# Issuing the loads of all later batches from GpSimd instead of SyncE, and reordering the first batch's hand-over

## The chip, the cores and the metric

The kernel runs on one core of one Trainium2 chip. The metric is device time in microseconds (us) of one execution. Three runs of the kernel before gave 276.81, 277.83 and 279.06 us; the median, 277.83 us, is the time before.

The engines are named as in the profile: PE is TensorE's matrix multiplier and PEld its weight load, DVE is VectorE, ACT is ScalarE, POOL is GpSimd, SP is SyncE. A "q" behind a name (SPq, POOLq) is the engine's instruction queue, from which it also issues transfers. Transfers that SP issues run in the hardware queue q1, transfers that POOL issues in the software queue q0; both share the same 16 DMA engines.

## What is computed

A linear attention with cosine weights, and then a mixer that mixes over positions and over channels. There are 8 batches of 8 heads, 576 positions and 64 elements per head.

```python
def phi(x, c, s):                       # c, s: cos and sin of pi/2 * position / 576
    r = np.maximum(x, 0.0)
    return np.concatenate([r * c, r * s], axis=-1)
q_p, k_p = phi(q, cos_w, sin_w), phi(k, cos_w, sin_w)
kv  = einsum('bhsf,bhsd->bhfd', k_p, v)
num = einsum('bhsf,bhfd->bhsd', q_p, kv)
den = einsum('bhsf,bhf->bhs', q_p, k_p.sum(axis=2)) + 1e-06
x = (num / den)                         # heads side by side: (8, 576, 512)
h = relu(x^T @ w_tok1) @ w_tok2         # over positions, 256 wide
u = x + h^T
out = u + relu(u @ w_ch1) @ w_ch2       # over channels, 1536 wide
```

All inputs and the output are float32; the kernel multiplies in bfloat16.

## The kernel before

**Tiles.** The 576 positions of a batch are four chunks of 128 (0 to 3) and a tail of 64, called chunk R (4). Two batches share the 128 partitions of a tail tile, so the tail's features, u and channel part are computed for both batches of a pair at once, with the odd one. The chunks of a batch are worked in the order 0, 1, 2, R, 3 (`ORDER`).

**Two halves of the work.** `Front` holds what a batch needs up to u: features of k and q (`feature`, line 264, on DVE), values cast to bfloat16 (`values`, lines 275 and 277), the products kv (`kv`, line 321), the turned query features (`q_trans` with PE for the first two batches, `q_trans_dma`, line 353, a transposing transfer from SP, for the others), the numerators (`num`, line 362), the token mixer (`tok1`, line 385, and `tok2`, line 409), and the turning of u (`u_trans_dma`, line 438, and `tail_trans_dma`, line 443, transfers from SP). `Channel` holds the channel mixer: 12 steps of `c_main` (line 531) with `c_tail` (line 551) in odd batches, and then the steps of `o_step` (line 564), two of the 12 blocks of `w_ch2` at a time.

**Order of the work.** The order is written by hand: every engine takes its instructions in program order, and waits only for data and for buffers that are still in use. While `Channel(b)` runs through its steps, the pieces of `Front(b + 1)` are put between them: `pieces` makes a list of (step, piece). Step C + i is the i-th of the 12 `c_main` steps, O + i the i-th `o_step` behind them. For a batch from the third on, chunks' query features and their transposes stand at steps C + 1 to C + 5, the numerators at C + 8 to O + 3, then the mixer and the transposes of u. The first batch is worked alone (`first_front`), and the second batch's pieces, which use PE transposes, stand between the channel steps of the first (`first` in `pieces`, lines 468 to 481). There the last piece list holds the query transposes of chunks 2, R, 3 with three of the first batch's `tok2` between them, the casts of v (two on POOL, two on ACT, one on DVE) and kv.

**Loads.** A main load of k, v or q of a batch is 1,024 KB (`load_main`, line 86), a load of a tail 128 KB (`load_tail`, line 92). Main tiles have two buffers (`io`, `bufs=2`), so batch b + 2 goes where batch b was. `load_batch` issues them on SP: those of batch 1 at the start, the first of them behind the second of the `w_ch1` loads (an added dependency, `after`); k and v of batch 2 at step 12 of the first channel behind the second `w_ch2` load, and q of it 16 steps later; in steady state v and q of batch b + 2 at step 5 of channel b, and k of batch b + 3 at step 24 (step 30 for b = 0). As SP takes its instructions in order, they go out only when the transposes and stores that stand ahead of them in the program have gone out. An even batch brings the tails of its pair with it. The weights `w_ch1` and `w_ch2` are loaded from POOL, which casts them on the way (lines 188 and 194); `w_ch2` waits for q of batch 1. The stores are issued by SP (lines 571 and 575).

Of the kernel before, what the change touches and what calls it, by code (L numbers as in the profile page):

```python
# [16 lines left out]
def kernel(  # L17
# [15 lines left out]
    nc = tc.nc  # L33

    B, H, S, D = q.shape
# [4 lines left out]
    P = 128  # L40
    R = S // P
# [5 lines left out]
    NCH = D_ch // P  # L47
# [9 lines left out]
    def half(g):  # L57
        return slice(g * ST, (g + 1) * ST)
# [19 lines left out]
    def after(later, earlier):  # L78
        tc.add_manual_dep(later.ins, earlier.ins.name,
                          mybir.DependencyInfo(mybir.DependencyClass.Sync,  # L80
                                               mybir.DependencyReason.DATA),
                          reason="order of the first loads")


    def load_main(dst, src, b, lo=0, hi=H, eng=nc.sync):
        return eng.dma_start(
            out=dst[:, lo:hi, 0:R * D].rearrange("p h (r d) -> p h r d", r=R),
            in_=src[b, lo:hi, 0:SM, :].rearrange("h (p r) d -> p h r d", r=R))


    def load_tail(dst, src, b):
        return nc.sync.dma_start(out=dst[half(b % 2)],
                                 in_=src[b, :, SM:S, :].rearrange("h s d -> s h d"))

    def tiles():
        return tuple(io.tile([P, H, R * D], F32, name=n) for n in ("qt", "vt", "kt"))

    def tail_tiles():
        return tuple(io.tile([P, H, D], F32, name=n) for n in ("qtt", "vtt", "ktt"))
# [4 lines left out]
    load_main(qt0, q, 0, 0, HH)  # L104
    load_main(qt0, q, 0, HH, H, nc.scalar)
    load_tail(qtt0, q, 0)
    load_main(kt0, k, 0, 0, HH)
    k_done = load_main(kt0, k, 0, HH, H)
    load_tail(ktt0, k, 0)
    load_main(vt0, v, 0, 0, HH)  # L110
    load_tail(vtt0, v, 0)
    load_main(vt0, v, 0, HH, H)

# [11 lines left out]
    w_ch2 = const.tile([P, NCH, Dm], BF16, name="w_ch2")  # L125
# [59 lines left out]
    w_ch1_done = []  # L185
    for c2 in range(2):
        for ki in range(0, NCC, 2):
            w_ch1_done.append(nc.gpsimd.dma_start(
                out=w_ch1[:, ki:ki + 2, c2 * C2:(c2 + 1) * C2],
                in_=moe_w_ch1[ki * P:(ki + 2) * P, c2 * C2:(c2 + 1) * C2]  # L190
                .rearrange("(n c) d -> c n d", c=P)))
    after(w_ch1_done[0], k_done)
    def load_w_ch2(behind):
        done = [nc.gpsimd.dma_start(
            out=w_ch2[:, ki:ki + 4, :],
            in_=moe_w_ch2[ki * P:(ki + 4) * P, :].rearrange("(n t) d -> t n d", t=P))
            for ki in range(0, NCH, 4)]
        after(done[0], behind)
        return done

# [14 lines left out]
    class Front:  # L217
# [243 lines left out]
        def pieces(self, b, before):  # L461


            first, odd = b == 1, b % 2 == 1
            V, KV, N = self.values, self.kv, self.num
            KS, QS, QT, T = self.k_side, self.q_side, self.q_trans, self.tok2
            C, O = 0, NCH
            if first:

                last = NCH - 1  # L470
                plan = [(4, KS, 0), (5, KS, 1, True), (6, KS, 2, True), (6, KS, 3, True), (7, KS, R),
                        (8, QS, 0), (9, QS, 1), (9, QT, 0), (10, QS, 2), (10, QT, 1)]
                plan += [(last, *what) for what in (
                    (QS, 3, True), (QT, 2, (0, H), nc.vector), (before.tok2, 2, None, False),
                    (QS, R, True), (QT, 3), (before.tok2, 3, None, False),
                    (QT, R, (0, H), nc.vector), (before.tok2, R, None, False))]
                plan += [(last, V, ci, eng) for ci, eng in enumerate(
                    (nc.gpsimd, nc.gpsimd, nc.scalar, nc.scalar, nc.vector))]
                plan += [(last, KV, ci) for ci in range(NSC)]
                plan.append((last, self.kv_out))  # L480
                plan += [(5, before.tok2, 0, ps_at, False), (7, before.tok2, 1, ps_at, False)]
            else:
                plan = [(C + at, V, ci, nc.scalar) for ci, at in enumerate((-1, -1, 0, 1, 2))]
                plan += [(C + at, KS, ci) for ci, at in enumerate((0, 0, 1, 2, 2))
                         if ci < R or not odd]
                for ci, at in zip(ORDER, (1, 2, 3, 4, 5)):
                    if ci < R or not odd:
                        plan += [(C + at, QS, ci), (C + at, self.q_trans_dma, ci)]

                plan += [(C + at, KV, ci) for ci, at in  # L490
                         enumerate((2, 3, 4, 5, 6) if odd else (2, 3, 4, 6, 7))]
                plan.append((C + (6 if odd else 7), self.kv_out))
            if first:
                at, mix, t = (O + 1, O + 3, O + 5, O + 7, O + 9), O + 10, O + 14
            elif odd:
                at, mix, t = (C + 8, C + 9, C + 11, O + 1, O + 3), O + 4, O + 8
            else:
                at, mix, t = (C + 9, C + 10, C + 11, O + 1, O + 3), O + 4, O + 8
            plan += [(i, N, ci) for i, ci in zip(at, ORDER)]
            plan += [(mix, self.mix_head, 0), (mix + 1, self.mix_head, 1),  # L500
                     (mix + 2, self.mix_tail)]

            plan += [(t + at, T, ci) for ci, at in enumerate((0, 1, 2, 3, 3) if not first else
                                                             (0, 0, 1, 2, 2))]
            plan += [(t + 3 - first, self.u_trans_dma, 3, R)]
            plan.append((t + 2 - first, self.u_trans_dma, 0, 3))
            if odd:
                plan.append((t + 3 - first, self.tail_trans_dma))
            slots = {}
            for slot, what, *args in sorted(plan, key=lambda p: p[0]):  # L510
                slots.setdefault(slot, []).append((what, args))
            return slots
# [183 lines left out]
                c.c_block(mi, kb)  # L696
        return c

    def load_batch(b, which="kvq", behind=None):
        if b not in io_tiles:  # L700
            io_tiles[b] = tiles()
        if b // 2 not in io_tails:
            io_tails[b // 2] = tail_tiles()
        qt, vt, kt = io_tiles[b]
        qtt, vtt, ktt = io_tails[b // 2]
        done = []
        for n in which:
            dst, tail_dst, src = {"k": (kt, ktt, k), "v": (vt, vtt, v), "q": (qt, qtt, q)}[n]
            done.append(load_main(dst, src, b))
            if behind is not None and len(done) == 1:  # L710
                after(done[0], behind)
            if b % 2 == 0:
                load_tail(tail_dst, src, b)
            if b % 2 == 0 or b == 1:
                load_tail(tail_dst, src, b | 1)
        return done


    results = [dict() for _ in range(B)]
    done = load_batch(1, "kqv", behind=w_ch1_done[1])  # L720
    w_ch2_done = load_w_ch2(done[1])
    tails = {0: tail0}
    f = Front(0, results[0], tail0)
    c = first_front(f)
    for b in range(B):
        slots = {}
        if b + 1 < B:
            if (b + 1) // 2 not in tails:
                tails[(b + 1) // 2] = Tail((b + 1) // 2)
            slots = Front(b + 1, results[b + 1], tails[(b + 1) // 2]).pieces(b + 1, f)  # L730
        if b > 0:
            c = Channel(b, results[b], tails[b // 2])
        for what, args in slots.pop(-1, ()):
            what(*args)
        for i, step in enumerate(c.steps(AHEAD if b == 0 else 0)):
            step()
            for what, args in slots.pop(i, ()):
                what(*args)


            if b == 0 and i == NCH:
                load_batch(2, "kv", behind=w_ch2_done[1])
            if b == 0 and i == NCH + 16:
                load_batch(2, "q")
            if 0 < b < B - 2 and i == NSC:
                load_batch(b + 2, "vq")
            if b < B - 3 and i == NCH + (18 if b == 0 else 12):
                load_batch(b + 3, "k")
        assert not slots
# [32 lines left out]
```

## Time and profile before

| what | value |
|---|---|
| runs (median; lowest, highest) | 277.83 us; 276.81, 279.06 |
| profiled execution | 275.45 us, of which the span of the profile is 273.6 |
| granted clock of PE | 1.0 of full speed, in all 40 slices |
| PE busy | 261.6 us, 96% of the span, 2050 matmuls |
| DVE, ACT, POOL busy | 164.7, 129.8, 11.2 us |
| DMA queue q1 (from SP) | 49.62 MB, 65.4% of 16 engines' span |
| DMA queue q0 (from POOL) | 3.21 MB, 7.1% |

PE's busy time is a poor gauge here: the rows give a 128x512 matmul about 379 ns, but back to back they start every 216 ns. What PE loses shows as distance between starts beyond that. The stages of the span are: the first batch's front to about 26 us, the first channel with the second batch's pieces to about 60 us, and from there one channel in each 27 to 34 us, the last of which ends at 270 us and is followed by the last stores.

### The profile page before, as it was taken

What the parts mean: (1) busy time and instruction counts of PE and PEld (TensorE: products, weight loads), DVE (VectorE), ACT (ScalarE), POOL (GpSimd) and SP (SyncE); (2) the same over time, 40 slices, a digit from 0 to 9 for tenths busy, and PEclk for the clock granted to TensorE, in tenths of its full rate; (3) what the DMA queues carried; (4) which work ended last, traced back from release to release, by engine and by line L of the source; (5) the groups of instructions that cost most, each with busy time, mean ns of one, the idle gap of its engine ahead of it and who ended that gap; (6) DMA issues with size and microseconds to landing.
All of it is one profiled execution on the core that took longest, in us unless ns stands there. A gap on an engine that the chain in (4) does not pass through costs nothing.

```text
span 273.6 us, 5130 instructions
## 1 busy us (share of the span) xinstructions
PE 261.6 (96%) x2050; PEld 138.7 (51%) x2050; DVE 164.7 (60%) x375; ACT 129.8 (47%) x229; POOL 11.2 (4%) x24
## 2 busy tenths in 40 slices
PE   7989987999899999999999999999999999999994
PEld 2665354446554454445654455446644455435543
DVE  6973775774876396659566487659466577720022
ACT  4955982067525184156626183347606372426500
POOL 6400230000000000000000000000000000000000
PEclk9999999999999999999999999999999999999999
DMA  7999999738995897968993969669994361180032
GB/s 222 344 266 283 317 179 283 245 88 264 284 253 185 247 221 191 323 140 233 208 311 79 270 193 259 220 151 237 211 304 119 115 117 38 42 210 0 2 98 94
DMA packets 91816, 53.68 MB, mean 196 GB/s; under 512 B 59409, under 2 KB 86929, under 8 KB 91793
## 3 DMA queue, kind: packets, MB, share of 16 engines
q1 hardware_dynamic: 88432, 49.62, 65.4%
q0 software_dynamic: 2832, 3.21, 7.1%
q10 hardware_dynamic: 528, 0.52, 0.6%
q8 instruction: 16, 0.26, 0.4%
q14 instruction: 8, 0.06, 0.1%
HBM read 35.85 MB, written 9.44 MB: 166 GB/s over the span
## 4 chain that ended last, share of the span: by engine, by line
PE 80%; DMA 7%; DVE 7%; ACT 2%; issue 1%; SPq 0%; DVEq 0%
PE o_ps L564 31%; PE c_ps L531 23%; PE b_ps L385 6%; PE u_ps L409 5%; PE num_ps L362 4%; PE ct_ps L551 4%; DMA qpT<-qp 4%; PE kv_ps L321 3%; DVE qp L264 2%; DMA uT<-u_bf 2%; DMA qt<-in_q_dram 2%; DVE kp L264 2%; PE idle_ps L205 1%; PE c_ps L541 1%; DVE u_sb L412 1%
## 5 line engine op out<-in xcount | busy, mean ns | idle before, releaser
L564 PE MATMUL o_ps<-w_ch,h1T 128*128 128x512 bf16 (+1 forms) x396 | 94.8, 372 | 0.0
L531 PE MATMUL c_ps<-uT,w_ch 128*128 128x512 bf16 (+2 forms) x384 | 91.6, 372 | 1.0 <-DMA uT<-u_bf 1.0
L535 ACT ACTIVATE h1T<-c_ps 128x512 bf16<-128x512 f32 x93 | 55.4, 598 | 57.1 <-PE c_ps L531 56.9
L564 PEld LDWEIGHTS <-h1T 128*128 128x128 bf16 x396 | 37.0, 97 | 38.8
L531 PEld LDWEIGHTS <-w_ch 128*128 128x128 bf16 x384 | 33.3, 97 | 31.2 <-DMA uT<-u_bf 2.0
L569 DVE TENSOR_TENSOR o_sb<-o_ps,u_sb 128x512 f32<-128x512 f32 (+1 forms) x33 | 22.2, 673 | 32.7 <-PE o_ps L564 32.7
L412 DVE TENSOR_TENSOR u_sb<-u_ps,x_sb 128x512 f32<-128x512 f32 x32 | 22.0, 689 | 7.3 <-PE u_ps L409 6.8
L416 ACT CAST u_bf<-u_sb 128x512 bf16<-128x512 f32 x28 | 17.3, 618 | 17.8 <-DVE u_sb L412 16.1
L390 ACT ACTIVATE B<-b_ps 128x512 bf16<-128x512 f32 x8 | 4.8, 597 | 39.5 <-PE b_ps L385 39.5
L409 PE MATMUL u_ps<-B,w_tok 128*128 128x512 bf16 x80 | 22.5, 379 | 0.0
L372 DVE TENSOR_TENSOR x_sb<-num_ps,den 128x512 bf16<-128x512 f32 x28 | 19.4, 691 | 1.0
L551 PEld LDWEIGHTS <-w_ch 128*128 128x128 bf16 x192 | 14.0, 98 | 9.2
L264 DVE TENSOR_SCALAR qp<-qt,cos_t 128x512 bf16<-128x512 f32 (+1 forms) x35 | 15.9, 453 | 4.6 <-DMA qt<-in_q_dram 4.6
L385 PE MATMUL b_ps<-x_sb,w_tok 128*128 128x512 bf16 x64 | 17.9, 379 | 0.0
L264 DVE TENSOR_SCALAR kp<-kt,cos_t 128x512 bf16<-128x512 f32 x32 | 15.2, 480 | 3.9 <-DMA kt<-in_k_dram 3.9
L551 PE MATMUL ct_ps<-uT_tail,w_ch 128*128 128x128 bf16 x192 | 17.2, 219 | 0.0
L275 ACT CAST v_aug<-vt 128x512 bf16<-128x512 f32 (+1 forms) x30 | 16.7, 586 | 0.1
L264 DVE TENSOR_SCALAR qp<-qt,sin_t 128x512 bf16<-128x512 f32 (+1 forms) x34 | 15.7, 460 | 0.0
L362 PEld LDWEIGHTS <-qpT 128*128 128x128 bf16 x256 | 11.5, 98 | 7.1 <-DMA qpT<-qp 1.5
L362 PE MATMUL num_ps<-kv_sb,qpT 128*128 128x65 bf16 x256 | 13.1, 193 | 1.7 <-DMA qpT<-qp 0.7
L569 DVE TENSOR_TENSOR o_sb<-o_ps,u_tail 128x512 f32<-128x512 f32 x4 | 2.8, 692 | 20.0 <-PE o_ps L564 20.0
L321 PE MATMUL kv_ps<-v_aug,kp 128*128 128x65 bf16 x256 | 12.5, 193 | 2.2 <-ACT v_aug L275 1.7
(96 smaller groups left out, 220.9 us busy)
## 6 DMA issues: line engine op xcount, KB each, us to landing
out_dram<-o_sb SPq DMA_DIRECT2D x31, 256.0 KB, 2.9
kt<-in_k_dram SPq DMA_DIRECT2D x7, 1024.0 KB, 6.9
qt<-in_q_dram SPq DMA_DIRECT2D x7, 1024.0 KB, 8.6
vt<-in_v_dram SPq DMA_DIRECT2D x7, 1024.0 KB, 6.5
w_ch<-in_moe_w_ch_dram POOLq DMA_DIRECT2D x4, 384.0 KB, 10.4
w_ch<-in_moe_w_ch_dram POOLq DMA_DIRECT2D x3, 512.0 KB, 8.3
out_dram<-o_sb SPq DMA_DIRECT2D x10, 128.0 KB, 2.3
qtt<-in_q_dram SPq DMA_DIRECT2D x8, 128.0 KB, 5.9
```

Of the source, the lines that this page charges most:

```text
L264: nc.vector.tensor_scalar(o_ap, i_ap, scalar1=w, scalar2=0.0, op0=ALU.mult, op1=ALU.max)
L321: nc.tensor.matmul(self.kv_ps[g][:, j * DP:j * DP + D1], self.k_of(ci)[:, g * HH + j, :, :] .rearrange("p a b -> p (a b)"), self.va[:, ci, ...
L362: nc.tensor.matmul(num_ps[:, g, j * DP:j * DP + D1], self.qT_of(ci, h), self.kv_sb[g][:, j, 0:D1], start=True, stop=True)
L372: nc.vector.tensor_mul(self.x_of(ci)[rows].rearrange("p (g j d) -> p g j d", g=2, j=HH), nv[:, :, :, 0:D], den.to_broadcast([rows.stop - r ...
L385: nc.tensor.matmul(self.b1_ps[mi], w, self.x_of(ci), start=(ci == ORDER[0]), stop=(ci == ORDER[-1]))
L409: nc.tensor.matmul(u_ps, w_tok2[:, ki, ci * P:(ci + 1) * P], self.B1[:, ki, :], start=(ki == 0), stop=(ki == NT - 1))
L412: nc.vector.tensor_add(u, u_ps[rows], self.x_of(ci)[rows])
L531: nc.tensor.matmul(c_ps[:, lo:hi], w_ch1[:, ki, mi * P:(mi + 1) * P], uT[:, lo // P:hi // P, ki, :], start=(ki == 0), stop=(ki == NCC - 1))
L535: nc.scalar.activation(self.h1T[:, mi, :], c_ps, AF.Relu)
L551: nc.tensor.matmul(self.ct_ps[:, mi % R, :], w_ch1[:, ki, mi * P:(mi + 1) * P], self.tail.uT[:, ki, :], start=(mi % R == 0 and ki == 0), s ...
L564: nc.tensor.matmul(o_ps, h, w_ch2[:, ki, cols], start=ki == 0, stop=ki == NCH - 1)
L569: nc.vector.tensor_add(o_sb, o_ps, u)
```

## The change

- `load_batch` issues every load of batches 1 to 7, tails too, on POOL's queue. SP keeps the loads of batch 0, two weight loads, all transposes and all stores.
- The three added dependencies of these loads go: k of batch 1 behind the second `w_ch1` load, `w_ch2` behind q of batch 1, and k of batch 2 behind the second `w_ch2` load. On POOL's queue they follow each other in program order. The dependency of the first `w_ch1` load on k of batch 0 stays.
- q of batch 2 is issued with k and v of it, 16 steps earlier in the program.
- For the second batch, the query transposes of chunks 0 and 1 move from steps 9 and 10 behind step 11, so that all stand behind the first batch's `tok2` of chunks 2 and 3; the first batch's `tok2` of its tail moves behind kv; four chunks of v are cast on POOL (two before), none on ACT; chunk 1's and 3's transposes are copied out on DVE.
- For batches 3, 5 and 7 (counted from 0), the numerators of chunks 2, R and 3, the mixer and u's transposes stand one step earlier.

```diff
-    def load_tail(dst, src, b):
-        return nc.sync.dma_start(out=dst[half(b % 2)],
+    def load_tail(dst, src, b, eng=nc.sync):
+        return eng.dma_start(out=dst[half(b % 2)],
...
-    def load_w_ch2(behind):
...
-        after(done[0], behind)
+    def load_w_ch2():
...
                 plan = [(4, KS, 0), (5, KS, 1, True), (6, KS, 2, True), (6, KS, 3, True), (7, KS, R),
-                        (8, QS, 0), (9, QS, 1), (9, QT, 0), (10, QS, 2), (10, QT, 1)]
+                        (8, QS, 0), (9, QS, 1), (10, QS, 2), (10, QS, 3, True)]
                 plan += [(last, *what) for what in (
-                    (QS, 3, True), (QT, 2, (0, H), nc.vector), (before.tok2, 2, None, False),
-                    (QS, R, True), (QT, 3), (before.tok2, 3, None, False),
-                    (QT, R, (0, H), nc.vector), (before.tok2, R, None, False))]
-                plan += [(last, V, ci, eng) for ci, eng in enumerate(
-                    (nc.gpsimd, nc.gpsimd, nc.scalar, nc.scalar, nc.vector))]
+                    (QS, R, True), (before.tok2, 2, None, False), (before.tok2, 3, None, False),
+                    (QT, 0), (QT, 1, (0, H), nc.vector), (QT, 2), (QT, 3, (0, H), nc.vector),
+                    (V, R, nc.vector), (QT, R, (0, H), nc.vector))]
+                plan += [(last, V, ci, nc.gpsimd) for ci in range(R)]
                 plan += [(last, KV, ci) for ci in range(NSC)]
-                plan.append((last, self.kv_out))
+                plan += [(last, self.kv_out), (last, before.tok2, R, None, False)]
...
             elif odd:
-                at, mix, t = (C + 8, C + 9, C + 11, O + 1, O + 3), O + 4, O + 8
+                at, mix, t = (C + 8, C + 9, C + 10, C + 11, O + 2), O + 3, O + 7
...
-            done.append(load_main(dst, src, b))
-            if behind is not None and len(done) == 1:
-                after(done[0], behind)
+            load_main(dst, src, b, eng=nc.gpsimd)
             if b % 2 == 0:
-                load_tail(tail_dst, src, b)
+                load_tail(tail_dst, src, b, nc.gpsimd)
             if b % 2 == 0 or b == 1:
-                load_tail(tail_dst, src, b | 1)
+                load_tail(tail_dst, src, b | 1, nc.gpsimd)
...
-    done = load_batch(1, "kqv", behind=w_ch1_done[1])
-    w_ch2_done = load_w_ch2(done[1])
+    load_batch(1, "kqv")
+    load_w_ch2()
...
             if b == 0 and i == NCH:
-                load_batch(2, "kv", behind=w_ch2_done[1])
-            if b == 0 and i == NCH + 16:
-                load_batch(2, "q")
+                load_batch(2, "kvq")
```

More of the change, by code (lines that the diff above doesn't have):

```diff
@@ L192 @@
     after(w_ch1_done[0], k_done)
-    def load_w_ch2(behind):
[L194 to L197, printed above, removed]
-        after(done[0], behind)
-        return done
+    def load_w_ch2():
+        for ki in range(0, NCH, 4):
+            nc.gpsimd.dma_start(
+                out=w_ch2[:, ki:ki + 4, :],
+                in_=moe_w_ch2[ki * P:(ki + 4) * P, :].rearrange("(n t) d -> t n d", t=P))
     def busy(dst, times):
@@ L697, in first_front, with load_batch @@
         return c
-    def load_batch(b, which="kvq", behind=None):
+    def load_batch(b, which="kvq"):
         if b not in io_tiles:
@@ L705, in load_batch @@
         qtt, vtt, ktt = io_tails[b // 2]
-        done = []
         for n in which:
             dst, tail_dst, src = {"k": (kt, ktt, k), "v": (vt, vtt, v), "q": (qt, qtt, q)}[n]
-            done.append(load_main(dst, src, b))
-            if behind is not None and len(done) == 1:
-                after(done[0], behind)
+            load_main(dst, src, b, eng=nc.gpsimd)
             if b % 2 == 0:
-                load_tail(tail_dst, src, b)
+                load_tail(tail_dst, src, b, nc.gpsimd)
             if b % 2 == 0 or b == 1:
-                load_tail(tail_dst, src, b | 1)
-        return done
+                load_tail(tail_dst, src, b | 1, nc.gpsimd)
     results = [dict() for _ in range(B)]
-    done = load_batch(1, "kqv", behind=w_ch1_done[1])
-    w_ch2_done = load_w_ch2(done[1])
+    load_batch(1, "kqv")
+    load_w_ch2()
     tails = {0: tail0}
```

## The prediction

> **What bounds the kernel now.** I read the stretches by stage first, to see where PE is short of work, then PE's waits, then the chain of work, and last the transfers of single windows. PE's clock is 1.0 throughout, so it plays no part.
>
> ```profile
> 28.00:49.00 21.00, 17.89 (x172) 10.03 (x171) 15.22 (x35) 13.46 (x22) 3.88 (x5) 1.00 1.11 263
> 49.00:77.00 28.00, 26.44 (x229) 14.92 (x228) 19.02 (x42) 14.31 (x26) 0.00 (x0) 1.00 0.79 214
> 77.00:238.00 161.00, 160.87 (x1181) 82.60 (x1178) 105.94 (x237) 73.83 (x131) 0.00 (x0) 1.00 0.73 196
> ```
>
> The columns are the stretch, its length, and PE's busy time first. From 77 to 238 us PE lacks 0.13 us. There the kernel is bound by PE's own work, and better transfers can win almost nothing. What can be won lies in 28 to 77 us (3.1 + 1.6 us idle). The waits and the chain name the causes:
>
> ```profile
> PE kv_ps L321 <- ACT v_aug L275: 1.7, 1, 1.7
> PE qT_ps L343 <- DVE qp L264: 1.3, 2, 0.7
> PE c_ps L531 <- DMA uT<-u_bf: 1.0, 2, 0.6
> PE num_ps L362 <- DMA qpT<-qp: 0.7, 1, 0.7
> ```
> ```profile
> 42.38 1.05 ACT v_aug L275 x2
> 57.21 3.30 DMA uT<-u_bf
> 68.25 5.41 DMA qpT<-qp
> 100.74 4.42 DMA qpT<-qp
> ```
>
> The reader sees one stall on ACT's casts of v, some on query features, and transposes that the chain holds as late. A transpose lands a median 3.0 us after its issue; the one of 68.25 took 5.41, behind k of batch 3 in q1 (issued at 64.05, landed at 71.57).
>
> **Time base.** The profiled execution took 275.45 us (span 273.6 and 1.85 around it), 2.38 below the median of 277.83. Differences are worked out on its trace and added to the median.
>
> **What the change saves.** (1) In the second batch's pieces PE's starts show 0.84 (34.44 us), 0.82 (38.76), 1.82 (42.95) and 0.28 us (43.47) of waiting: 3.8. With the transposes after `tok2` and the casts on POOL these go, but five PE transposes now follow each other through two PSUM buffers, each copied out in 1.0 us (ACT) or 0.69 (DVE): about 0.85 + 0.7 + 0.7 us of new waiting. Saved: 1.5. POOL's four casts take 4 x 0.72 = 2.9 us from v's landing (35.98), so to 38.9, before kv at about 40.8; this hides them by 1.9 us. (2) Batch 2's q lands at 67.28 because it is issued at 61.30; loaded early it removes 0.55 us (69.03) and 0.91 (73.70): 1.45. (3) u of the last batch a step earlier takes about 0.45 of the 0.78 us at 243.8. Sum: 3.4 us. SP loses 42 load issues of 0.4 to 3.6 us; PE is not waiting for them beyond (2).
>
> **What it adds: issue on POOL.** 21 tails at about 0.65 us and 21 main loads at about 1 us (estimates from POOL's own rows: 0.60 us for a load of 64 packets, 0.80 for 256, 0.83 for 512): some 35 us, on an engine with 11.2 us of work. Only the casts of v stand behind loads there, behind `w_ch2`. If POOL can't write the 6,000 packets of batch 1 and `w_ch2` ahead, the casts start only when the third `w_ch2` load is let in, up to 3 us after they are wanted; the trace shows no more than the 1,024 of `w_ch1` written ahead. The bounds are 0 and 3 us. I take 0, since PE has 1.9 us in hand there and what is ahead drains at the same time as v, and keep 3 for the range.
>
> **What it adds: loads that run ahead.** SP's order held the loads back: v and q of batch 5 went out at 134.71, behind the transposes of 126.71 to 133.40. POOL has nothing ahead of them but a free buffer. In channel b the buffers of batch b + 1 come free when its features are made: in channel 2, k at 99.67 and q at 102.04, v before. So k, v, q of batch b + 3, 3 MB (3.75 with tails), start in q0 at 101 us, just when batch b + 1's transposes of 98.95, 100.74, 102.1 and 103.4 are in q1. Before they met only an earlier load; now all but the first share the engines with 9 to 11 us of loads. This occurs in channels 1 to 4; channels 5 and 6 load nothing.
>
> How the two queues share: here both had long rows of packets, and transposes alone:
>
> ```profile
> q0 software_dynamic: 167, 0.26, 62.2%
> q1 hardware_dynamic: 172, 0.38, 47.9%
> ```
> ```profile
> GB/s 272 127 18 94 0 0 0 0 0 0 214 152 246 269 257 255 164 44 18 18 18 9 0 0 0 3 9 6 12 9 9 9 12 9 20 260 284 287 295 281
> q1 hardware_dynamic: 1199, 0.30, 92.5%
> q8 instruction: 1, 0.02, 2.4%
> ```
>
> The first fence is 14.75 to 17 us: 167 packets against 172, one for one whatever their size. The second is 101 to 104.5 us: one 16 KB packet of another queue (1.4 us on one engine) takes the whole transpose stream from 270 GB/s to about 10. [...]
>
> A transpose is 1,024 rows of 256 B, 64 on each engine at 18 ns: 1.15 us. A 1 KB load packet takes 46 ns. One for one, a transpose takes 64 x 64 ns = 4.1 us; unslowed 1.15. I take 3 rows per 2 load packets, 3.1 us: near the one-for-one row, the only one with two full queues, but less, as q0's packets first moved 1.4 to 4.2 us after issue and leave gaps. Channel 2, with transposes wanted by the numerators at 103.8, 104.9, 106.0 and 108.3 (the last two a step earlier than the 107.19 and 109.40 seen): the first lands unslowed at 101.8, the others at 105.45, 108.55, 111.65, so PE waits 0.55 + 2.0 + 0.8 = 3.35 us (each wait moves what follows). Channel 4 the same. Channels 1 and 3 have slack, since their numerators come later and tails' packets take only 18 ns: 1.55 each, all at chunk 3. Sum 9.8. Before that, batches 2 and 3 now queue behind `w_ch2` to about 64 us (6.75 MB at 330 GB/s from 44), so u's first transpose at 57 us, 96 rows, takes 4.7 us instead of 1.7: 2.9 more at the 0.6 us wait of 60.55. Total added 12.7; net 12.7 - 3.4 = +9.3: 287.1.
>
> [...]
>
> **The rivals.** A, the other side: transposes travel in long turns. If 16 rows (288 ns) go between 4 load packets (184 ns), a transpose takes 4 x 472 ns = 1.9 us; channel 2 waits 0.15, u 1.1, and the savings stand: -3.4 + 1.4 = -2.0, 275.8; with no slowing at all 274.4. It decides from 2.2 us per transpose downwards. For it: 256 B packets of q1 went several to one of q0 around 9 us; against it: the one-for-one window. B: strictly one for one: waits of 5.5, 5.5, 3.9, 3.9 and 4.4: +23.2 - 3.4 = 297.6. C: POOL's writing of packets blocks DVE's features. Seen: of nine around POOL's 2.48 us at 32.6, two took 0.6 instead of 0.48 us. That is 0.25 us; at a whole issue (0.8 us) for each of six features it is 4.8, less 1.65 us of slack, in 4 channels: +12.6 - 3.4 = 287. [...] D: late casts, A with 3 us more: 278.
>
> **How the numbers follow.** Forecast (transposes slowed, 279 to 296) 0.54; A 0.25; B and beyond 0.10; C 0.05; D 0.06. The time is the forecast's, 287.1; its own range 279 to 296. A range that leaves 2 in 10 out takes in A's near end and stops at B: 274.5 to 297.6. A difference under 1% can't be told from none (275.05 to 280.61). Faster: most of A, 0.20. Same: the rest of A, D, the forecast's low end, 0.18. Slower 0.62.
>
> **What would show it.** Right: transposes of channels 1 to 4 landing 4 to 9 us after issue, waits of numerators on them, loads of batch b + 3 in the first third of channel b, none of this in channels 5 and 6. PE's wait on ACT's v gone. Wrong: transposes at 3 us beside full q0 (A); loads that start only late in a channel, for POOL waits I overlooked; features at 1 us (C).

## The result and the profile after

The kernel after takes 326.17 us (median of its three fast runs, 324.71 to 327.41; 329.18 over all six, of which three, at 330.94 to 333.95, fell into a slower state that runs of any kernel can fall into) against 277.61 us before (6 runs, 275.97 to 279.06). The ratio is 1.175, 95% interval 1.167 to 1.183. The forecast was 287.1 us and its range ended at 297.6, so the sign was right and the size was not. The profiled execution took 326.17 us, of which the span is 324.0.

Here are the stretches by stage of the kernel after, the last one longer because the kernel is. Columns as before: stretch, length, busy time of PE, PEld, DVE, ACT and POOL, then PE's clock, the DMA share and GB/s.

```profile
28.00:49.00 21.00, 19.35 (x187) 11.14 (x185) 17.74 (x38) 11.92 (x19) 11.15 (x15) 1.00 1.10 289
49.00:77.00 28.00, 19.28 (x124) 10.04 (x122) 15.16 (x33) 9.29 (x17) 9.98 (x10) 0.82 1.06 290
77.00:290.00 213.00, 181.81 (x1272) 91.38 (x1271) 109.66 (x245) 79.80 (x143) 20.10 (x18) 0.91 0.57 136
```

The first stretch gained: PE is busy for 19.35 us of it where it was 17.89. The second lost 7.2 us of PE's work, and from 77 us on PE is idle for 31 us where it lacked 0.13. There is also something new in the clock's column: 0.82 and 0.91 where the kernel before shows 1.00. PE's waits, and POOL's longest one (who waited for what: total us, times, longest):

```profile
PE num_ps L360 <- DMA qpT<-qp: 20.0, 5, 6.8
PE num_ps L360 <- DMA qpT_tail<-qp_tail: 11.1, 2, 6.8
PE c_ps L528 <- DMA uT<-u_bf: 8.7, 1, 8.7
PE qT_ps L341 <- ACT qpT L345: 1.1, 1, 1.1
```
```profile
POOL kt L86 <- DVE kp L262: 117.9, 4, 38.0
```

PE's wait on ACT's casts of v is gone, and in its place are 1.1 us on a copy out of PSUM, where this kernel's matmuls write. All other new waits above 0.5 us are for transposes. POOL's longest waits, 117.9 us in all, are for a free buffer, as foreseen; its others are 6 us or less. The chain of waits (start, length, what) holds the same transposes, now 11 to 21 us long where those shown of before took 3.3 to 5.4:

```profile
76.76 13.67 DMA qpT_tail<-qp_tail
...
117.07 11.43 DMA qpT<-qp
...
158.21 20.84 DMA qpT<-qp
...
206.01 14.16 DMA qpT<-qp
```

The transfers of 122 to 129 us, in the second half of the second of these, by queue (packets, MB, share of 16 engines' time):

```profile
q0 software_dynamic: 620, 2.40, 93.2%
q1 hardware_dynamic: 625, 0.15, 10.6%
```

The reader sees three things. The queues share one packet for one, 620 to 625 (some 30 of each are of 4 B). A packet of q0 is 2.40 MB / 620 = 3.9 KB, and takes 0.932 x 16 x 7 us / 620 = 168 ns; a row of q1 takes 19 ns. And 625 rows in 7 us make 7 x 1024 / 625 = 11.5 us for one transpose. The packet records give most of q0's packets 4,096 B and 164 ns, and 64 x (18 + 164) ns is 11.6 us. The forecast had 3.1.

Between PE's matmul starts I count 41.6 us of waiting on transposes: 8.9 us for u (ended 67.5), 4.8 in channel 1 (84.9 and 90.5), 7.25 in channel 2 (120.5 and 128.55), 14.0 in channel 3 (170.1 and 179.1), 6.65 in channel 4 (214.7 and 220.2), and none in channels 5 and 6. Behind the six waits of 4.5 us and more, 128x512 matmuls start every 427 ns instead of 216 (behind the first, 128x384 ones every 320 instead of 163), for 1.3 to 5.1 us each; this loses another 11.0 us in these large matmuls, 12.7 with the small ones. The page's clock row shows the same dips:

```profile
PEclk9999999859959998799985599959999999999999
```

### The profile page after: what moved, and what is told of

The parts are those of the page before. It is cut to its first block, busy times and chain, and to the rows that moved or that the text cites. A ratio compares the mean times of both kernels' runs of the same rounds, so it can differ in the third digit from the quotient of the medians.

```text
span 324.0 us, 5146 instructions
## 1 busy us (share of the span) xinstructions
PE 276.5 (85%) x2050; PEld 143.9 (44%) x2050; DVE 166.0 (51%) x376; ACT 127.6 (39%) x226; POOL 58.3 (18%) x68
## 4 chain that ended last, share of the span: by engine, by line
PE 72%; DMA 19%; SPq 3%; DVE 3%; ACT 1%; issue 1%; POOL 0%; POOLq 0%
PE o_ps L561 29%; PE c_ps L528 19%; DMA qpT<-qp 14%; PE b_ps L383 6%; PE u_ps L407 5%; DMA qpT_tail<-qp_tail 4%; PE idle_ps L203 3%; SPq L351 3%; PE num_ps L360 3%; PE kv_ps L319 2%; PE ct_ps L548 2%; PE qT_ps L341 1%; DVE kp L262 1%; PE c_ps L538 1%; DVE qp L262 1%
## 5 line engine op out<-in xcount | busy, mean ns | idle before, releaser
L528 PE MATMUL c_ps<-uT,w_ch 128*128 128x512 bf16 (+2 forms) x384 | 95.7, 385 | 8.7 <-DMA uT<-u_bf 8.7
L561 PE MATMUL o_ps<-w_ch,h1T 128*128 128x512 bf16 (+1 forms) x396 | 99.8, 388 | 0.0
L561 PEld LDWEIGHTS <-h1T 128*128 128x128 bf16 x396 | 38.6, 101 | 42.6 <-issue 5.0
L528 PEld LDWEIGHTS <-w_ch 128*128 128x128 bf16 x384 | 34.5, 101 | 40.3 <-DMA uT<-u_bf 9.2
L86 POOL DMA_DIRECT2D kt<-in_k_dram x7 | 15.7, 2245 | 118.2 <-DVE kp L262 117.9
L360 PE MATMUL num_ps<-kv_sb,qpT 128*128 128x65 bf16 x256 | 13.9, 200 | 21.0 <-DMA qpT<-qp 20.0
L368 DVE TENSOR_SCALAR den<-num_ps 128x8 f32<-128x8 f32 (+1 forms) x35 | 5.8, 166 | 50.5 <-PE num_ps L360 50.4
L360 PEld LDWEIGHTS <-qpT 128*128 128x128 bf16 x256 | 11.9, 102 | 28.3 <-DMA qpT<-qp 23.1
L383 PE MATMUL b_ps<-x_sb,w_tok 128*128 128x512 bf16 x64 | 19.9, 415 | 0.0
L548 PEld LDWEIGHTS <-w_ch 128*128 128x128 bf16 x192 | 14.0, 98 | 9.2
L262 DVE TENSOR_SCALAR qp<-qt,cos_t 128x512 bf16<-128x512 f32 (+1 forms) x35 | 16.2, 462 | 0.6 <-DMA qt<-in_q_dram 0.6
L273 ACT CAST v_aug<-vt 128x512 bf16<-128x512 f32 (+1 forms) x28 | 15.7, 589 | 0.1
```

What stands on the lines that cost most here:

```text
L262: nc.vector.tensor_scalar(o_ap, i_ap, scalar1=w, scalar2=0.0, op0=ALU.mult, op1=ALU.max)
L360: nc.tensor.matmul(num_ps[:, g, j * DP:j * DP + D1], self.qT_of(ci, h), self.kv_sb[g][:, j, 0:D1], start=True, stop=True)
L383: nc.tensor.matmul(self.b1_ps[mi], w, self.x_of(ci), start=(ci == ORDER[0]), stop=(ci == ORDER[-1]))
L528: nc.tensor.matmul(c_ps[:, lo:hi], w_ch1[:, ki, mi * P:(mi + 1) * P], uT[:, lo // P:hi // P, ki, :], start=(ki == 0), stop=(ki == NCC - 1))
L548: nc.tensor.matmul(self.ct_ps[:, mi % R, :], w_ch1[:, ki, mi * P:(mi + 1) * P], self.tail.uT[:, ki, :], start=(mi % R == 0 and ki == 0), s ...
L561: nc.tensor.matmul(o_ps, h, w_ch2[:, ki, cols], start=ki == 0, stop=ki == NCH - 1)
```

## The experiments

My theory after the result (T): GpSimd's loads of batch b + 3 run beside the transposes of batch b + 1, q0's packets are 4 KB, the queues take turns packet by packet, and so a transpose takes some 11 us; the long waits then halve PE's clock. Rivals: the new order of the work is the cause (O); GpSimd's own work or queue is, by something other than its packet size (G).

**Keep the change, take the collision away.** The first load of each group from batch 3 on waits for the last transpose issued ahead of it. Nothing else changes.

```diff
+    turned = []
...
+            turned.append(nc.sync.dma_start_transpose(...))
...
-            load_main(dst, src, b, eng=nc.gpsimd)
+            done = load_main(dst, src, b, eng=nc.gpsimd)
+            if at == 0 and turned:
+                after(done, turned[-1])
```

> The changed kernel, with all loads from batch 3 on still issued by GpSimd, but the first of each group held until the last transpose issued ahead of it has landed. Theory T (turns): two queues take turns packet by packet on each DMA engine, and a packet of GpSimd's loads is 4,096 B (164 ns) against a transpose's row of 256 B (18 ns), so a transpose beside loads lands 10 us late; without the overlap transposes land about 3 us after issue, the waits of 41.6 us and the half clock of 11 us behind them go, and the time is 273 to 277 us. [...]

Measured: 274.09 us (272.12 to 274.82); ratio to before 0.988, interval 0.985 to 0.992. PE's waits on transposes in it, its last long stretch, and POOL's longest wait:

```profile
PE num_ps L362 <- DMA qpT<-qp: 0.8, 2, 0.4
PE c_ps L530 <- DMA uT<-u_bf: 0.7, 1, 0.7
```
```profile
77.00:238.00 161.00, 160.16 (x1163) 81.96 (x1162) 106.08 (x233) 74.34 (x132) 19.68 (x25) 1.00 0.76 195
```
```profile
POOL vt L86 <- DMA qpT<-qp: 41.2, 3, 15.2
```

POOL now waits for transposes, where nothing depends on it, and PE does not. The whole loss is gone, half clock included. The two profiled executions differ by 326.17 - 274.02 = 52.15 us; the waits (41.6 less the 1.5 left here) and the half clock (11.0) explain 51.1 of them, or 52.8 with the small matmuls at half clock. It also shows what the rest of the change is worth: 277.15 - 274.09 = 3.06 us.

**The new order alone.** The loads stay on SP as before; only the order of the second batch's pieces and the earlier step for odd batches are taken over.

```diff
-                        (8, QS, 0), (9, QS, 1), (9, QT, 0), (10, QS, 2), (10, QT, 1)]
+                        (8, QS, 0), (9, QS, 1), (10, QS, 2), (10, QS, 3, True)]
...
-                at, mix, t = (C + 8, C + 9, C + 11, O + 1, O + 3), O + 4, O + 8
+                at, mix, t = (C + 8, C + 9, C + 10, C + 11, O + 2), O + 3, O + 7
```

> The kernel before, with only the reordering of the change: second batch's query transposes behind u of the first, casts of v on GpSimd, numerators, mixer and u of batches 3, 5 and 7 one step earlier. Loads as before from SyncE. Theory T: the order is not the cause; 1.2 us saved in the first channel as seen in the changed kernel, 0.4 at the last u, and up to 1 us lost where a transpose of batches 3 to 7 is now wanted a step earlier: 275.5 to 278 against 277.6. Rival O: over 300 us.

Measured: 275.61 us (274.28 to 276.93), ratio 0.993 (0.990 to 0.996). O falls: the order by itself gains 1.5 us. Waits of 0.5 and 1.15 us on batch 2's q (69.5 and 74.5 us) remain, since q still comes late. Behind two new waits on PSUM copies, of 1.3 and 1.5 us, the profiled execution was also at half clock from 40.9 to 44.3 us.

**The loads alone.** Before, with only the loads moved to GpSimd, q of batch 2 early with them, and their three dependencies dropped.

```diff
-            done.append(load_main(dst, src, b))
+            load_main(dst, src, b, eng=nc.gpsimd)
```

> The kernel before, with only the loads moved to GpSimd (q of batch 2 early and the three dependencies gone with them); order of the pieces as before. Theory T: the same overlap, numerators of batches 3, 5, 7 wanted a step later, so some 1 us less wait in each: 322 to 332 us. Rival O: back to within 5 us of 277.

Measured: 327.13 us in the profiled run; a second took 338.75. PE's waits in it:

```profile
PE num_ps L360 <- DMA qpT<-qp: 26.4, 6, 8.7
PE num_ps L360 <- DMA qpT_tail<-qp_tail: 7.5, 2, 6.4
PE c_ps L529 <- DMA uT<-u_bf: 7.1, 2, 6.7
PE kv_ps L319 <- ACT v_aug L273: 1.7, 1, 1.7
```

Here the loss stands alone, 41 us of it on transposes, beside the old wait on ACT's casts.

**Transfers by themselves.** No arithmetic at all: four transposes of 256 KB each beside three loads of 1,024 KB, once for every way to issue the loads, each phase behind the last one.

```diff
+    phases = [
+        lambda: [turns()],
+        lambda: [loads(nc.gpsimd, plain)],
+        lambda: [loads(nc.gpsimd, plain), turns()],
+        lambda: [loads(nc.gpsimd, padded), turns()],
+        lambda: [loads(nc.gpsimd, cast), turns()],
+        lambda: [loads(nc.scalar, plain), turns()],
+        lambda: [loads(nc.sync, plain) + turns()],
+        lambda: [turns()],
+    ]
```

> Computes nothing: it writes zeros to the output and then runs eight phases of transfers, each behind the landing of the one before: four 256 KB transposes from SyncE alone; three 1,024 KB loads from GpSimd alone; transposes beside such loads from GpSimd; beside loads from GpSimd into rows padded by 64 B; beside loads from GpSimd that cast to bfloat16; beside loads from ScalarE's queue; loads and then transposes in SyncE's one queue; transposes alone again. Theory T: alone 4 transposes land within 7 us of the first issue; beside plain GpSimd loads they land only when the loads have, at 12 to 14 us; the cast loads have packets of one 1 KB row (about 59 ns each by w_tail's row), so a transpose takes about 64 x 77 ns = 4.9 us; beside ScalarE's queue, packets of 1 KB (46 ns), 64 x 64 ns = 4.1 us each; in one queue they land behind the loads at about 14 us. The padded loads tell whether 4,096 B packets come from merged destinations (then 4.1 us each) or from framing by GpSimd (then as plain). Rival P: the two queues share by bytes, and transposes land at about twice their time alone whatever the packets.

Measured, from the first issue to the landings: alone, four transposes take 7.3 us, landing 1.2 to 1.4 us apart. Beside GpSimd's plain loads (issued 51.8) they land at 57.6, 66.3, 67.1 and 67.9, the loads at 59.6, 62.7 and 65.9: one transpose gets through while the loads run, and the second is still under way when they end. Padding the destination rows, so that no two touch, changes nothing: the packets stay 4,096 B. With GpSimd casting to bf16, transposes land at 89.0, 93.4, 97.7 and 101.1, some 4 us apart; with ACT's hardware queue at 108.8, 112.7, 115.2 and 116.2, at most 3.8 apart. In SP's one queue they land behind the loads, at 129.4 to 132.9 (the last load at 128.5). The queues of the plain, the casting and the ACT case, from 58 to 64, 86 to 100 and 105 to 112 us:

```profile
q0 software_dynamic: 519, 1.99, 94.9%
q1 hardware_dynamic: 518, 0.13, 10.7%
```
```profile
q0 software_dynamic: 3098, 1.57, 86.1%
q1 hardware_dynamic: 2930, 0.73, 39.6%
```
```profile
q10 hardware_dynamic: 1933, 1.95, 81.4%
q1 hardware_dynamic: 1934, 0.48, 31.3%
```

Bytes over packets give 3.8 KB, 0.5 KB and 1.0 KB, and the queues go about one for one in all three. At the pace of 58 to 64 us a transpose takes 6 x 1024 / 518 = 11.9 us beside plain loads. The same data cut by GpSimd into casting packets of 512 B (62 ns each) lets one through every 4.3 us, and a hardware queue with 1 KB every 3.8. What a transpose costs follows the neighbour's packet: in the casting case GpSimd issues the same loads in the same queue, so G is not needed for it. The casting and the hardware case come out a little under the plain sum (4.3 against 4.9, and 3.8 against 4.1 expected): the two shares add up to 126% and 113%, so times of different queues overlap a little.

**The same in the kernel.** The kernel after, with GpSimd casting the main loads of batches 1 to 7 to bf16 tiles; its packets become small, and nothing is held back. Batch 0 keeps float32 tiles of its own.

```diff
-        return tuple(io.tile([P, H, R * D], F32, name=n) for n in ("qt", "vt", "kt"))
+        return tuple(io.tile([P, H, R * D], BF16, name=n) for n in ("qt", "vt", "kt"))
```

> The changed kernel, with main loads of batches 1 to 7 cast to bfloat16 on the way (the features and values are then made of bfloat16 inputs; batch 0 stays float32). Same queue, same early start, but GpSimd's packets become single rows of 1 KB read and 512 B written, 59 ns, where 4,096 B took 164. Theory T: a transpose beside them takes about 4.3 us, as in the measurement of the queues, not 10 or more; waits per channel of 4 to 6 us in channels 1 to 4 become about what the prediction's case B has, some 20 us in all with u's transpose; with half clock behind some: 293 to 305 us. Rival P (any load beside, by bytes or by path): as before the cast, 320 us or more. A transpose at 3 us and a time of 277: both are wrong.

Measured: 307.34 us (306.46 to 308.22), ratio 1.108 (1.101 to 1.114), 2.3 us above T's range and below P's 320. PE's waits on transposes, and the queues from 114 to 120 us:

```profile
PE num_ps L361 <- DMA qpT<-qp: 16.0, 4, 5.9
PE c_ps L529 <- DMA uT<-u_bf: 5.5, 1, 5.5
PE num_ps L361 <- DMA qpT_tail<-qp_tail: 5.3, 1, 5.3
```
```profile
q0 software_dynamic: 1449, 0.73, 88.4%
q1 hardware_dynamic: 1451, 0.36, 46.7%
```

Small packets give back some 19 of the 52 us (326.17 - 307.34), at the same early start and with the same engine issuing; DVE's features, which now read bfloat16, also take 0.35 to 0.37 us instead of 0.48. Both queues go one for one, and 6 x 1024 / 1451 makes 4.2 us for a transpose, as T has it. They do not give back all, for two reasons that T left out. The casting loads are slower, and so are met for longer (in the transfers by themselves the last of three landed 15.0 us after its issue, the last plain one 11.8). And a transpose issued beside such loads is slow to start: the one of 107.09 us moved its first row at 112.11, 5.0 us later, and u's transpose in the kernel after 4.0 us after its issue, where alone it takes 1.2. So the four that this run's chain holds still land 10.4 to 16.2 us after issue. What delays the start is not shown.

**One collision alone.** The gate, but only from batch 4 on, so that u's transpose of batch 1 meets the loads of batch 3 again.

```diff
-            if at == 0 and turned:
+            if at == 0 and turned and b > 3:
```

> Like e1_gate, but the loads of batch 3 are not held back, so that one collision of the changed kernel comes back alone: u's transpose of batch 1 beside the 3 MB of batch 3. Theory T (each collision costs its own wait and the half clock behind it): the wait of the changed kernel at 67.5 us (8.9 us) and some 1.9 us of half clock, 10.8 us over e1_gate's 274.1, so 283 to 286 us; PE waits 7 to 9 us on uT near 60 to 68 us, all other waits on transposes stay below 1 us. Rival (the waits of the changed kernel feed each other, each late transpose making the next collision worse): alone the wait is under 5 us, and the time 276 to 281.

Measured: 282.43 us (281.56 to 283.53), ratio 1.017 (1.014 to 1.021), 0.6 us below T's interval and above the rival's. PE's waits and the chain of this kernel:

```profile
PE c_ps L530 <- DMA uT<-u_bf: 6.7, 1, 6.7
```
```profile
58.06 9.58 DMA uT<-u_bf
```

The transpose lands at 67.6 us, as in the kernel after (67.5); PE only reaches it 2.2 us later than there and so waits 6.9 instead of 8.9, for in this profile it was also at half clock from 40.75 to 44.16 us, before the collision (the lines stand in the next experiment). With 1.85 us of half clock behind it that is 8.7, and the medians differ by 282.43 - 274.09 = 8.3. So one collision costs its own wait and half clock, and the collisions need not feed each other. I had not foreseen that the wait itself is 2 us shorter here.

**Is it the idle time that halves the clock?** Filler matmuls ahead of six of the waits, so that PE is not idle. They add some 37 us of work that is thrown away.

```diff
+    FILL = {(2, R): 50, (3, 2): 80, (4, R): 80, (4, 3): 80, (5, 2): 65}
...
+            fill = fill or FILL.get((self.b, ci), 0)
...
+            if self.b == 1 and mi == 0 and lo == 0:
+                busy(c_ps, 38)
```

> The changed kernel, with matrix products of zeros put on TensorE ahead of the six places where it waited 4.5 to 8.9 us for a transpose (4 to 8 us of filler each, written to PSUM columns that are not used or are overwritten). If the half clock behind the waits (11 us in the changed kernel) is TensorE's answer to standing idle, the waits for transposes stay late as they were, but the clock stays at 1.0 and 8 to 11 us go: 316 to 320 us against 327. If the clock falls for another reason, or filler lengthens the way, the time stays at 325 or above.

Measured: 337.93 us (334.61 to 338.15; a fourth run took 343.76). The expectation was missed, and the run settles little. The waits fell only to about 21 us, as transposes of the channels behind landed later still (one took 17.2 us from issue, 119.96 to 137.12); why is not shown. The loss to half clock fell from 12.7 to 7.4 us, small matmuls included, but the waits had become shorter as well.

The better form of the question: the gated kernel, with no collision, and ahead of chunk 0's numerators of batches 2 to 6 a chain of copies on ACT for which PE has to wait.

```diff
+    IDLE = {2: 4, 3: 6, 4: 8, 5: 10, 6: 12}
...
+            if ci == 0 and self.b in IDLE:
+                for n in range(IDLE[self.b]):
+                    nc.scalar.copy(hold, held)
+                nc.tensor.matmul(num_ps[:, 0, HH * DP:512], hold[:, 0:P], zeros[:, 0:512 - HH * DP],
+                                 start=True, stop=True)
```

> Like e1_gate, with no collision; instead, ahead of the numerators of chunk 0 of batches 2 to 6, a chain of 4, 6, 8, 10 and 12 copies of 128x512 on ACT of some 0.6 us each, for which PE waits through one small added matmul (192 columns of zeros, overwritten by the numerators). So PE gets five idle stretches of growing length, some 2 to 7 us, with the DMA engines nearly idle. Theory T (it is PE's idle time that halves the clock): behind the shorter ones, up to about 3 us, matmuls start every 216 ns at once; behind the longer ones every 427 ns for 1 to 4 us. Rival (the half clock comes from the load of the DMA engines or from power): no half clock behind any of them.

Measured in one run of 315.44 us: waits of 3.57, 4.73, 6.17, 7.33 and 8.77 us. The 5 us behind each of them (PE's busy time, clock, DMA share, GB/s):

```profile
74.94:79.94 5.00, 5.00 (x31) 0.50 0.58 193
112.53:117.53 5.00, 5.00 (x34) 0.50 0.85 267
151.60:156.60 5.00, 5.00 (x39) 0.60 0.99 390
191.03:196.03 5.00, 5.00 (x34) 0.50 0.97 360
232.70:237.70 5.00, 5.00 (x32) 0.52 0.46 184
```

All five are at about half clock, the shortest like the longest, and the loss is 1.2 to 2.0 us each in the 128x512 matmuls, whatever the wait's length. PE waited for ACT here and for no transfer, so it is idle time that does it and not what PE waited for. The DMA engines were not nearly idle, as I had planned (shares of 0.46 to 0.99), so against their load as the cause stand other stretches: the kernel before is at full clock from 28 to 49 us with a share of 1.11.

My chains came out longer than planned, so this run does not say how long a wait must be. The expectation's 3 us was an estimate; the kernel after shows only the full clock behind waits of 0.8 and 1.1 us, and half of it behind those of 4.5 us and more. The traces together say that no length of a single wait decides. In the clock records of the kernel after the changes lie whole steps of 3.41 us apart (61.93, 72.17, 89.24, 96.06, 126.78 us and so on; in the run with one collision the steps lie elsewhere, at 40.75 and 44.16), and what goes with a change is PE's busy time within the step before it. In the kernel after, from 20 us on, the clock fell from full to half behind steps with 0 to 0.34 us of busy time and behind none with 1.66 us or more (that much from 119.96 to 123.37); it came back behind steps with 3.41 us, and not behind one with 2.30 (177.98 to 181.40). In the ten profiled kernels (all but the transfers by themselves) the most behind which it fell was 1.48 us (the filler run, 218.41 to 221.82), and the least behind which it did not was 1.56 us (the gated kernel, 37.78 to 41.19). So two waits of 1.3 and 1.6 us in one step were enough in the run with one collision, which has these two steps (PE's busy time, clock, DMA share, GB/s):

```profile
37.34:40.75 3.41, 0.83 (x13) 1.00 1.23 221
40.75:44.16 3.41, 3.40 (x46) 0.50 1.03 329
```

A single wait of 1.92 us (loads alone, 221.3 us) was not enough, and one of 2.1 us (filler, 221.2 us) was. The full clock returned 4.0 to 5.6 us after the waits of this run (4.2 to 5.7 us after those of the kernel after), at the end of the first step that PE worked through. A step need not be idle throughout: 1.93 of the 3.41 us were enough in the filler run. This is read out of the traces; no run was made to try it.

**A better version?** The gated kernel with the first batch's `tok2` put between the second batch's query transposes, against the new waits on PSUM copies.

```diff
-                    (QS, R, True), (before.tok2, 2, None, False), (before.tok2, 3, None, False),
-                    (QT, 0), (QT, 1, (0, H), nc.vector), (QT, 2), (QT, 3, (0, H), nc.vector),
+                    (QS, R, True), (before.tok2, 2, None, False), (QT, 0),
+                    (QT, 1, (0, H), nc.vector), (before.tok2, 3, None, False), (QT, 2),
+                    (before.tok2, R, None, False), (QT, 3, (0, H), nc.vector),
```

> The gated kernel of the first series (274.09 us), with the first batch's u products of chunks 2, 3 and the tail put between the second batch's query transposes instead of ahead of them and behind kv. There the five transposes waited 1.29, 1.22 and 0.50 us for PSUM buffers to be copied out; 3 x 0.43 us of products between them would cover up to 1.3 us, if VectorE, which also adds u (0.69 each), does not fall behind: 272.5 to 274. If VectorE is the limit there: 274 to 275.5.

Measured: 273.7 us (273.27 to 275.94; a sixth run took 277.83), ratio 0.988 (0.983 to 0.992): the same as the gated kernel. A wait of 1.4 us on DVE's copy stays in its list, so DVE's copies, with other work ahead of them in DVE's order, set this place. The best version found is the gated one, 274 us.

## Why the forecast was wrong in size

Its steps, in its own order:

| step of the forecast | foreseen, us | measured, us |
|---|---|---|
| second batch's pieces, first stage | -1.5 | -1.24 (`o_ps` starts at 42.71, before 43.95) |
| batch 2's q early, u a step earlier | -1.9 | -1.8 (rest of the gated kernel's -3.06) |
| POOL's issue, casts of v behind loads | 0 (0 to 3) | 0 (casts done at 38.7, forecast 38.9) |
| u's transpose, total wait | 3.5 | 8.9 |
| channels 1, 2, 3, 4 | 1.55, 3.35, 1.55, 3.35 | 4.8, 7.25, 14.0, 6.65 |
| channels 5, 6 | 0 | 0 |
| clock | 0 ("plays no part") | 11.0 |

The split of the second row is not measured. The gated kernel against the new order alone (275.61 - 274.09 = 1.5) should be what loads on GpSimd bring, and is close to the 1.45 given to q; but the new order alone lost about 1.4 us to half clock from 40.9 to 44.3 us in its profiled execution and the gated kernel nothing, so this agreement may be luck.

**Right:** where the savings come from and their sum (3.4 against 3.06), that POOL runs ahead because only a free buffer holds it, which transposes meet which loads, and that channels 5 and 6 are spared. The row that it read as one packet for one was read rightly too, though the sum then did not go by it.

**The step that failed** is "A 1 KB load packet takes 46 ns. One for one, a transpose takes 64 x 64 ns = 4.1 us", and "I take 3 rows per 2 load packets, 3.1 us" behind it. 1 KB is the packet of the same loads in SP's hardware queue; moved to GpSimd they come in packets of 4,096 B and 164 ns. The sum took the sharing from one queue's row and the packet from another's. The row of before that it showed held a warning: q0's 167 packets took 62.2% of 16 engines in 2.25 us, 134 ns each, three times what I used. With 64 x (18 + 134) ns = 9.7 us for a transpose, the same working would have ended above 297.6. Going below the one-for-one row ("3 rows per 2 load packets") then made it worse: the share was 620 to 625, and a transpose took 11.5 us instead of 3.1.

The slack that the forecast gave channels 1 and 3 went with it. Channel 3, foreseen as one of the cheap ones, lost most: its tail's transpose (issued 156.9) and chunk 3's (158.2) landed at 170.05 and 179.05, the latter with the end of all 3.75 MB. At 11 us a transpose, the end of the loads decides, not the order of the numerators.

**What was left out** is that a wait of this length costs more than itself. That PE's clock was 1.0 before said only that before had no long wait. 11.0 us, a fifth of the loss, came this way. Left out too is the slow start beside loads, 4.0 us to u's first row instead of 1.2.

**The rivals.** A (long turns) and D (late casts with it) are refuted by 11.5 us a transpose and casts done at 38.7 (D's own sum gives 278.8, not 278); no run shows A's turns of 16 rows and 4 load packets: in the kernel after one packet went for one, 620 to 625. C (POOL blocking DVE) is refuted: in the kernel after, the 36 features of 128x512 that ran while POOL was issuing loads took 480.5 ns on average, the 84 others 482.5. B had the rule right, strictly one for one, and fell short by the same 1 KB. What stays open: why a whole transpose stream slows beside one 16 KB packet (19 of its rows took 1.2 to 1.7 us each beside that of 101.9 us in the kernel before), what delays a transpose's first row beside loads, and what sets the clock, whose steps were read from traces alone.

## What to carry to other kernels

A queue whose order looks like a restriction may be what keeps transfers apart: when loads move to a queue of their own, ask what they will meet once only a buffer holds them, and put the old order back as a dependency where it costs nothing (here one wait on POOL turned +17.5% into -1%). Price sharing with the packet that the new issuer will make, bytes over packets and time over packets of that very queue. Price a long wait with what follows it: behind every wait of 3.57 us and more here PE's clock was halved, and the large matmuls lost another 1.2 to 2.5 us (0.6 where the next wait follows at once).

## What the runs showed of the hardware that was not expected

- GpSimd's plain loads of 1 KB rows go out in packets of 4,096 B (164 ns), with padded destination rows too (175 ns); its casting loads in single packets of 512 B (59 ns by the packet records); the same loads from SP or ACT in packets of 1,024 B (46 ns).
- A 256 KB transpose lands 2.7 to 2.8 us after issue alone, and a transpose of query features beside GpSimd's plain loads 9.7 to 20.8 us after it.
- A transpose of 256 KB moves its first row 1.2 us after issue alone, and 4.0 to 5.0 us after it when issued beside GpSimd's loads.
- A wait of 3.57 to 8.9 us leaves PE at half clock for up to 5.7 us; the loss of 1.2 to 2.5 us in large matmuls (0.6 where the next wait follows at once) does not grow with the wait. The changes of the clock lie whole steps of 3.41 us apart; it fell to half behind steps in which PE was busy for 0 to 1.48 us, and behind none with 1.56 us or more.
